# The order of work in a two-layer attention and GLU kernel: a list for two steps, maxima in halves, the transposed maxima ahead of PV, wo's products in the filler

## The chip, the core and the metric

The kernel runs on one core of one Trainium2 chip. The metric is the device time of one execution in microseconds. Three executions of the kernel before took 2374.63, 2372.8 and 2376.28 us, so the median is 2374.63 us. A core has TensorE for matrix products (PE in the profile, with its weight loads listed as PEld), VectorE (DVE), ScalarE (ACT), GpSimd (POOL) and SyncE (SP), which here only issues transfers. Each engine takes its instructions in the order in which the program lists them; an instruction that waits holds up what stands behind it on its engine.

## The reference

Two layers, each of attention with sixteen query heads and one key and value head, and of a gated unit. S is 2048, D 448, a head 28 wide, F 1792.

```python
def _A_ref(x, wq, wk, wv, wo):
    q = (x @ wq).reshape(B, S, H, Dh).transpose(0, 2, 1, 3)
    k = x @ wk
    v = x @ wv
    scores = jnp.einsum("bhqd,bkd->bhqk", q, k) * (Dh ** -0.5)
    p = _softmax(scores, axis=-1)
    o = jnp.einsum("bhqk,bkd->bhqd", p, v)
    return o.transpose(0, 2, 1, 3).reshape(B, S, H * Dh) @ wo
...
x = A_x
x = x + _A_ref(_layernorm(x), A_wq, A_wk, A_wv, A_wo)
x = x + _B_ref(_layernorm(x), B_w_gate, B_w_up, B_w_down)   # (sigmoid(x wg) * (x wu)) wd
x = x + _A_ref(...)
x = x + _B_ref(...)
```

## The kernel before

A unit u is 128 queries; a layer has 16 units. For each unit the kernel goes over 16 blocks of 128 keys, and one such block is a **step**, so that a layer has 256 steps and the program 512. I number steps from 0 in each layer.

In a step, `scores` (L485) makes four products `s`, one for each group of four heads, into one bank of PSUM each, and ACT writes the exponential `P` of each. `pv` (L494) multiplies the four `P` of the step before by the values (`pv`, summed over the 16 steps of the unit). Softmax needs the maximum over all keys of each query and head before a unit's first score, so `mx_gen` (L442) runs ahead: its group of four products `mx` (L458) takes one group of heads against 512 keys, and DVE reduces each of the four banks to a column of `mp` (L462). Sixteen groups make a unit. Then DVE reduces `mp` to `m32` and scales it to `m16` (L471, L472), and `fin` (L474) turns `m16` with TensorE (`mt`, L477), copies it (`mr`, L479) and stores it as a row of the unit's queries `QS`, from which the scores take it as a further term of the product. `fin` is put on the list `late`; with LT = 1 it runs in the same call of the generator that made `m16`, ahead of the next group's first product.

What TensorE does besides is **filler**: a list of generators (`Filler`, L727) with the query projections (`qp`), the gated unit's products (`gp`, `up`, `dn`) and, run whole and not in slices, a unit's output projection `wo` (twelve products, `fc`, L584) and the key and value projection (`kv`). `slice` (L743) first calls `flush`, which emits work that was deferred (evictions and the like), then adds nanoseconds to a debt and emits products until their estimated cost has paid it. The main loop sets `rate` in each step: what is left of the filler over the steps until it must be done.

The order inside a step is a string:

```python
    ORDER = "FSFSFSFSPXM"
    MORE = (5, 10)
```

F is a slice of the filler with a quarter of `rate`, S one score, P the products with the values, M one group of maxima (two in steps 5 and 10 of a layer's first unit), and X calls `tick`, which starts the next stage of the work that follows a unit: f0 to fb (sums, reciprocals and scaling through DRAM and POOL), `fc` with `wo`, then layer norm (fd), its transposed copy (fe) and the block's filler (ff). `fc` runs inside `tick` by `fill.run`, so its twelve products stand between P and M.

PSUM tiles of the pool `psf` share seven banks: `s`, `mx`, `qp`, `gp`, `up`, `dn`, `wo`, `mt` and `kv` all have the tag "f". `pv` has a bank of its own. A product into a bank waits until the tile that held it before was read.

Of the kernel before, what the change touches and what calls it, by code (L numbers as in the profile page):

```python
# [19 lines left out]
def interleaved_layers_kernel(ctx: ExitStack, tc: tile.TileContext, x, wq, wk, wv, wo, wg, wu, wd, out, layers=2):  # L20
# [421 lines left out]
    def mx_gen(l):  # L442

        load_qh(l, 0)
        for u in range(U):
            qh = QH[l, u]
            mp = wk1.tile([128, 4, 4, NB], F32, name="mp", bufs=2)
            for kb in range(NB):
                for g in range(G):
                    for i in range(len(late) - 1, -1, -1):  # L450
                        late[i][0] -= 1
                        if late[i][0] <= 0:
                            late.pop(i)[1]()
                    assert KVD[l] >= 4 * (kb + 1)
                    ps = [psf.tile([128, 512], F32, tag=BANKS["m"], name="mx", bufs=NBK[BANKS["m"]])
                          for _ in range(4)]
                    for h in range(4):
                        nc.tensor.matmul(ps[h], qh[32 * h:32 * h + 32, g],  # L458
                                         KK[l][32 * h:32 * h + 32, 1, kb * 512:(kb + 1) * 512], start=True,
                                         stop=True, tile_position=(32 * h, 0))  # L460
                    for h in range(4):
                        nc.vector.tensor_reduce(mp[:, g, h, kb:kb + 1], ps[h], axis=AX.X, op=OP.max)  # L462
                    ps = None
# [5 lines left out]
            m32 = wk1.tile([128, 16], F32, name="m32")  # L469
            m16 = wk1.tile([128, 16], F16, name="m16")  # L470
            nc.vector.tensor_reduce(m32, mp.rearrange("p g h k -> p (g h) k"), axis=AX.X, op=OP.max)  # L471
            nc.vector.tensor_scalar(m16, m32, -(2.0 ** -15), None, op0=OP.mult)  # L472

            def fin(u=u, m16=m16):  # L474
                stored.add(("m", l, u))
                p = fps([16, 128], F16, "mt")
                nc.tensor.transpose(p, m16, id16)  # L477
                r = wk1.tile([16, 128], F16, name="mr")
                nc.vector.tensor_copy(r, p)  # L479
                nc.gpsimd.dma_start(QS[l, u][28:29].rearrange("o g h n -> o (g h) n"), r)  # L480
            late.append([LT, fin])
# [44 lines left out]
    class Block:  # L526
# [8 lines left out]
        def tile(self, u):  # L535
# [47 lines left out]

            def fc():  # L584
                need(1)
                p = fps([128, D], F32, "wo")
                n = 0
                for h in range(4):
                    for a, c in ((0, 0), (0, 1), (1, 0)):
                        nc.tensor.matmul(p, v["oT"][:, a, h * 128:(h + 1) * 128], WO[:, c, h], start=n == 0, stop=n == 11)  # L590
                        n += 1
                        yield C448

                def f():
                    nc.vector.scalar_tensor_tensor(self.x1[:, t], p, osc, v["xr"], op0=OP.mult, op1=OP.add)
# [18 lines left out]
            def ff():  # L614
# [4 lines left out]
                        fill.add(qgen(l + 1, 1), G * QCH)  # L619
                return  # L620
                yield
            return (1, f0), (1, fx), (1, fy), (1, fz), (1, fw), (1, fa), (1, fb), (2, fc), (2, fd), (3, fe), (2, ff)

        def load_w(self, f):
            need(2 + f)
# [98 lines left out]
    QCH = 11 * C512  # L724
    BULK = FC * 22 * C256 + TB * 3 * FC * C448

    class Filler:  # L727
        def __init__(self):
            self.gens, self.debt = [], 0.0

        @property
        def left(self):
# [10 lines left out]
        def slice(self, ns):  # L743
            now[0] += 1
            flush()
            self.debt += ns
            while self.gens and self.debt > 0:
                g = self.gens[0]
                c = next(g[0], None)
                if c is None:  # L750
                    self.gens.remove(g)
                    continue
                self.debt -= c
                g[1] -= c
            if not self.gens:
                self.debt = min(self.debt, 0.0)

    fill = Filler()
# [65 lines left out]
    def first_mx():  # L824

        while QDONE.get((0, 0), 0) <= nmx % G and QDONE.get((0, 0), 0) < G:
            fill.slice(QCH / 2)
        next(mxs[0])

    for i in range(NT + L4):  # L830
        for k, f in st0:
# [38 lines left out]
    for l in range(layers):  # L870
# [10 lines left out]
        while late:  # L881
            late.pop(0)[1]()
        fill.slice(QCH)
        prevP = None
        rate = 0.0
        for step in range(U * KT):
            u, kt = divmod(step, KT)
            P = []
            for o in ORDER:
                if o == "S":  # L890
                    scores(l, u, kt, len(P), P)
                elif o == "M":
                    for _ in range(1 + (u == 0 and kt in MORE)):
                        next(mx, None)
                elif o == "P":
                    if prevP is not None:
                        pv(*prevP)
                elif o == "X":
                    if u and kt == 1:
                        b = (u - 1) // TB  # L900
                        if (l, b) not in BLK:
                            BLK[l, b] = Block(l, b)
                        later(*BLK[l, b].tile(u - 1))
                    if l == 0:
                        paced(step)
                    tick()
                    fed = sum(BLK[l, b].fed == TB for b in range(NBL) if (l, b) in BLK)
                    if fed < NBL - 1:
                        rate = fill.left / max(FIRST + TB * KT * fed - step, 1)
                    else:  # L910
                        rate = max(fill.left - KEEP, 0) / (U * KT - step)
                else:
                    fill.slice(rate / ORDER.count("F"))
            prevP = (l, u, kt, P)
        pv(*prevP)
# [5 lines left out]
        while (side or pend or fill.gens) if final else (side or pend or done < 4 * NB):  # L921
            tick()
            for _ in range(4):
                fill.slice(VS / 4)
            n += 1
            if not final and done < 4 * NB and QDONE.get((l + 1, 0)) == G and mx_ready(l + 1, done):
                if n >= 5 or done >= 4 * (NB - 1):
                    next(mxs[l + 1])
                    done += 1
                    n = 0  # L930

# [20 lines left out]
```

## Time and profile before

| what | value |
|---|---|
| median of three executions | 2374.63 us |
| span of the profiled execution, first to last instruction | 2370.5 us |
| steps 0 to 45 of layer 0 | 116.91 to 283.23 us |
| steps 46 to 255 of layer 0, up to the last steps | 283.23 to about 1133 us |
| the end of layer 0's units and blocks, start of layer 1 | about 1133 to 1284.45 us |
| steps 0 to 43 of layer 1 | 1284.45 to 1431.46 us |
| steps 44 to 255 of layer 1 | 1431.46 to 2283 us |
| the last blocks | 2283 us to the end |

The profile lists instructions of one execution with start and duration, and what ended the idle time before one, read from the semaphores. Its page gives no time of the profiled execution but its span; the 4.1 us between span and median lie before the first and after the last instruction, or are the spread between executions. A matrix product's listed duration contains the way through the array, so products that follow each other overlap: the time that one costs is the distance between starts.

### The profile page before, as it was taken

The page shows a single profiled execution, that of the slowest core. Times are in us where ns is not written, and L with a number is a line of the kernel's source. Part 1 is how long each engine was busy: PE and PEld are TensorE (multiplying, and loading weights), DVE is VectorE, ACT ScalarE, POOL GpSimd, SP SyncE. Part 2 cuts the span into 40 slices and gives each one's busy share as a digit, 9 for nine tenths or more (in the row PEclk, how much of TensorE's full clock was granted, in tenths as well). Part 3 has the DMA queues.
Part 4 walks back from the last instruction along what each step waited for, and adds up shares of the span by engine and source line. Part 5 has one row for each costly group of instructions (what it writes and reads, how often), then busy time and mean ns, then how long its engine had stood idle before and what let it go on. Part 6 is the DMA issues. An engine that isn't in the chain of part 4 may idle for free.

```text
span 2370.5 us, 40937 instructions
## 1 busy us (share of the span) xinstructions
PE 2226.5 (94%) x15592; PEld 990.3 (42%) x15592; DVE 1624.5 (69%) x2858; ACT 1560.6 (66%) x2583; POOL 348.7 (15%) x621
## 2 busy tenths in 40 slices
PE   3688899999999999999999989999999999999999
PEld 1221244444444444444573223444444444444456
DVE  3787787777767777774258887777677776777321
ACT  5497767676667767777513777767676776777751
POOL 5403565001111010101011011000000000000010
PEclk9899999999999999999999999999999999999999
DMA  5433563322223132322342112322232222222133
GB/s 145 132 115 95 155 197 111 102 85 71 90 70 108 55 101 85 91 94 63 108 136 57 27 49 82 95 63 87 62 106 63 89 63 91 86 81 93 57 109 120
DMA packets 227525, 218.57 MB, mean 92 GB/s; under 512 B 159408, under 2 KB 187760, under 8 KB 227328
## 3 DMA queue, kind: packets, MB, share of 16 engines
q1 hardware_dynamic: 220832, 200.11, 28.3%
q0 software_dynamic: 5376, 14.87, 1.7%
q8 instruction: 122, 2.00, 0.3%
q10 hardware_dynamic: 1120, 0.98, 0.1%
q14 instruction: 75, 0.61, 0.1%
HBM read 175.37 MB, written 23.59 MB: 84 GB/s over the span
## 4 chain that ended last, share of the span: by engine, by line
PE 78%; DVE 11%; ACT 3%; DMA 2%; issue 2%; SPq 1%; POOL 0%; ACTq 0%; DVEq 0%; POOLq 0%
PE pv L499 19%; PE s L488 16%; PE dn L680 11%; PE gp L334 10%; PE up L334 10%; DVE mp L462 8%; PE mx L458 6%; PE wo L590 3%; ACT P L491 2%; PE qp L334 2%; DVE st L289 0%; DMA qd<-qst 0%; DMA sums<-rc 0%; DMA lb<-sums 0%; DMA XT<-hl 0%
## 5 line engine op out<-in xcount | busy, mean ns | idle before, releaser
L491 ACT ACTIVATE P<-s,esc 128x512 f32<-128x512 f32 x2048 | 1309.2, 690 | 513.2 <-PE s L488 496.1
L462 DVE TENSOR_REDUCE mp<-mx 128x1 f32<-128x512 f32 x2048 | 1268.2, 683 | 408.0 <-PE mx L458 404.1
L488 PE MATMUL s<-QS,KK 96*128 96x512 f16 x2048 | 761.4, 382 | 61.8 <-DVE mp L462 41.1
L334 PEld LDWEIGHTS <-wgu 128*128 128x128 f16 x4928 | 458.1, 97 | 243.5 <-issue 96.8
L499 PE MATMUL pv<-P,VV 128*32 128x512 f32 x4096 | 549.2, 609 | 0.0
L334 PE MATMUL up<-XT,wgu 128*128 128x256 f16 x2464 | 375.6, 272 | 0.0
L334 PE MATMUL gp<-XT,wgu 128*128 128x256 f16 x2464 | 374.2, 273 | 0.2
L680 PE MATMUL dn<-WD,h 128*128 128x448 f16 x1344 | 321.7, 352 | 0.0
L488 PEld LDWEIGHTS <-KK 96*128 96x128 f16 x2048 | 193.1, 97 | 181.3 <-issue 107.9
L458 PE MATMUL mx<-KK,QH 32*128 32x512 f16 x2048 | 217.8, 389 | 17.3 <-DVE mp L462 5.3
L458 PEld LDWEIGHTS <-QH 32*128 32x128 f16 x2048 | 53.6, 91 | 396.8 <-issue 385.6
L680 PEld LDWEIGHTS <-h 128*128 128x128 f16 x1344 | 124.1, 98 | 135.8 <-issue 22.0
L499 PEld LDWEIGHTS pv<-P,VV 128*32 128x32 f32 x4096 | 81.0, 108 | 206.0 <-issue 193.9
L573 POOL TENSOR_TENSOR lb<-pvs,lb 128x512 f32<-128x512 f32 x32 | 40.5, 1265 | 789.0 <-DMA lb<-sums 647.5
L654 ACT ACTIVATE h<-th 128x512 f16<-128x512 f32 x112 | 70.4, 629 | 86.0 <-DVE th L651 85.8
L295 POOL TENSOR_SCALAR rs<-mv 128x1 f32<-128x1 f32 (+2 forms) x53 | 13.4, 252 | 702.4 <-DVE mv L290 691.6
L651 DVE SCALAR_TENSOR_TENSOR th<-th,up 128x512 f32<-128x512 f32 x112 | 76.1, 679 | 56.9 <-PE up L334 44.4
L334 PE MATMUL qp<-XT,WQ 128*128 128x512 f16 x352 | 108.7, 409 | 2.5 <-DVE mp L462 1.2
L655 DVE SCALAR_TENSOR_TENSOR h<-th,h 128x512 f16<-128x512 f32 x112 | 78.8, 703 | 46.1 <-ACT h L654 46.1
L643 ACT ACTIVATE th<-gp,gsc 128x512 f32<-128x512 f32 x112 | 76.9, 687 | 45.8 <-PE gp L334 45.8
L590 PE MATMUL wo<-WO,oT 128*128 128x448 f16 x384 | 78.3, 353 | 0.2 <-DVE oT L580 0.2
L334 PEld LDWEIGHTS <-WQ 128*128 128x128 f16 x352 | 34.0, 102 | 61.3 <-issue 38.8
(117 smaller groups left out, 787.8 us busy)
## 6 DMA issues: line engine op xcount, KB each, us to landing
wgu<-wgu_d SPq DMA_DIRECT2D x224, 512.0 KB
QS<-qd SPq DMA_DIRECT2D x384, 32.0 KB
lb<-sums SPq DMA_DIRECT2D x128, 64.0 KB
xr<-in_A_x_dram SPq DMA_DIRECT2D x32, 224.0 KB
qd<-qst POOLq DMA_DIRECT2D x28, 256.0 KB, 2.6
wgu_d<-sgu POOLq DMA_DIRECT2D x14, 512.0 KB, 3.8
QH<-qd SPq DMA_DIRECT2D x28, 128.0 KB
x2d<-x SPq DMA_DIRECT2D x16, 224.0 KB
```

Source lines behind the costliest of these rows:

```text
L334: nc.tensor.matmul(ps, a, b, start=n == 0, stop=n == 10)
L458: nc.tensor.matmul(ps[h], qh[32 * h:32 * h + 32, g], KK[l][32 * h:32 * h + 32, 1, kb * 512:(kb + 1) * 512], start=True, stop=True, tile_po ...
L462: nc.vector.tensor_reduce(mp[:, g, h, kb:kb + 1], ps[h], axis=AX.X, op=OP.max)
L488: nc.tensor.matmul(s, KK[l][0:96, 0, kt * 128:(kt + 1) * 128], QS[l, u][:, g].rearrange("p h n -> p (h n)"), start=True, stop=True)
L491: nc.scalar.activation(p, s, AF.Exp, scale=esc)
L499: nc.tensor.matmul(v[32 * g:32 * g + 32], VV[l][:, kt], P[g], start=kt == 0, stop=kt == KT - 1, tile_position=(0, 32 * g))
L590: nc.tensor.matmul(p, v["oT"][:, a, h * 128:(h + 1) * 128], WO[:, c, h], start=n == 0, stop=n == 11)
L643: defer(lambda: nc.scalar.activation(th, gp.rearrange("p j n -> p (j n)"), AF.Tanh, scale=gsc))
L651: nc.vector.scalar_tensor_tensor(t, th, 1.0, up.rearrange("p j n -> p (j n)"), op0=OP.add, op1=OP.mult)
L654: nc.scalar.activation(h[:, 0], t, AF.Copy, scale=2.0 ** -17)
L655: defer(lambda: nc.vector.scalar_tensor_tensor(h[:, 1], t, 2.0 ** -17, h[:, 0], op0=OP.mult, op1=OP.subtract), 1)
L680: nc.tensor.matmul(p, hs[f // 2][:, a, o:o + 128], WD[:, f, c], start=n == 0, stop=n == 3 * FC - 1)
```

## The change

The string becomes one of two, each for two steps, chosen by the rate when the pair begins:

```diff
-    ORDER = "FSFSFSFSPXM"
+    FULL = "FSFSFSFSTPXMFSFSFSFSTPXM"
+    LEAN = "FSFSmFSFSTPXmFSFSmFSFSTPXm"
+    PLAG = 1
+    LEANR = 600.0
...
+        while step < U * KT:
+            order = FULL if rate > LEANR else LEAN
+            for o in order:
...
                 elif o == "M":
-                    for _ in range(1 + (u == 0 and kt in MORE)):
-                        next(mx, None)
+                    group(mx)
+                elif o == "m":
+                    next(mx, None)
+                elif o == "T":
+                    finish()
                 elif o == "P":
-                    if prevP is not None:
-                        pv(*prevP)
+                    if len(PQ) > (sn % 4 == 0) * PLAG:
+                        pv(*PQ.pop(0))
                 elif o == "X":
+                    if u == 0 and kt in MORE:
+                        group(mx)
```

The maxima's generator now stops after two products and their reductions; `group` calls it twice. The unit's last reductions go with its sixteenth group, and the turning waits on `late` for T, which stands ahead of P:

```diff
+                    for hh in (0, 2):
+                        ps = {h: psf.tile([128, 512], F32, tag=BANKS["m"], name="mx", bufs=NBK[BANKS["m"]])
+                              for h in (hh, hh + 1)}
...
+                        if hh == 0:
+                            yield
...
+                    if kb * 4 + g == 15:
+                        maxima(l, u, mp)
                     yield
...
+    def maxima(l, u, mp):
+        m32 = wk1.tile([128, 16], F32, name="m32")
+        m16 = wk1.tile([128, 16], F16, name="m16")
+        nc.vector.tensor_reduce(m32, mp.rearrange("p g h k -> p (g h) k"), axis=AX.X, op=OP.max)
+        nc.vector.tensor_scalar(m16, m32, -(2.0 ** -15), None, op0=OP.mult)
...
+        late.append(fin)
+
+    def finish():
         while late:
-            late.pop(0)[1]()
+            late.pop(0)()
+
+    def group(m):
+        next(m, None)
+        next(m, None)
```

The output projection becomes a generator that stands first in the filler, and its later stages are put on the list when it has ended:

```diff
             def fc():
                 need(1)
+                fill.first.append(wo())
+                return
+                yield
+
+            def wo():
                 p = fps([128, D], F32, "wo")
...
                 defer(f)
+                later((2, fd), (3, fe), (2, ff))
...
+            for _ in range(DEAL):
+                while self.first:
+                    c = next(self.first[0], None)
+                    if c is not None:
+                        self.debt -= c
+                        break
+                    self.first.pop(0)
             while self.gens and self.debt > 0:
```

DEAL is 100, so that one slice takes all twelve products.

With the numbers that the program computes for `rate`, LEAN orders steps 0 to 45 of layer 0 and steps 0 to 43 of layer 1, and FULL all others. The lists of ACT and SP keep their order. Three places show what moves.

First place, TensorE in a lean step, step 30 of layer 1. Before, the scores stand together, and the values' products and four maxima's products follow:

```order
L488 LDWEIGHTS KK
L488 MATMUL s<-QS,KK 128x512
L488 LDWEIGHTS KK
L488 MATMUL s<-QS,KK 128x512
L499 MATMUL pv<-P,VV 32x512 x4
L458 LDWEIGHTS QH
L458 MATMUL mx<-KK,QH 128x512
L458 LDWEIGHTS QH
L458 MATMUL mx<-KK,QH 128x512
```

Now, from the second score of that step on:

```order
L497 LDWEIGHTS KK
L497 MATMUL s<-QS,KK 128x512
L455 LDWEIGHTS QH
L455 MATMUL mx<-KK,QH 128x512
L455 LDWEIGHTS QH
L455 MATMUL mx<-KK,QH 128x512
L497 LDWEIGHTS KK
L497 MATMUL s<-QS,KK 128x512
L497 LDWEIGHTS KK
L497 MATMUL s<-QS,KK 128x512
L508 MATMUL pv<-P,VV 32x512 x4
```

Two of the four products of the maxima moved from behind `pv` to between the second and the third score.

Second place, TensorE around an output projection in a full step, step 57 of layer 1. Before, the projection follows `pv`, and this is its end (the last of twelve products, then the maxima and the next step's score):

```order
L590 LDWEIGHTS oT
L590 MATMUL wo<-WO,oT 128x448
L458 LDWEIGHTS QH
L458 MATMUL mx<-KK,QH 128x512
L458 LDWEIGHTS QH
L458 MATMUL mx<-KK,QH 128x512
L458 LDWEIGHTS QH
L458 MATMUL mx<-KK,QH 128x512
L458 LDWEIGHTS QH
L458 MATMUL mx<-KK,QH 128x512
L488 LDWEIGHTS KK
L488 MATMUL s<-QS,KK 128x512
```

Now the beginning of the projection stands behind the same four products:

```order
L508 MATMUL pv<-P,VV 32x512 x4
L455 LDWEIGHTS QH
L455 MATMUL mx<-KK,QH 128x512
L455 LDWEIGHTS QH
L455 MATMUL mx<-KK,QH 128x512
L455 LDWEIGHTS QH
L455 MATMUL mx<-KK,QH 128x512
L455 LDWEIGHTS QH
L455 MATMUL mx<-KK,QH 128x512
L604 LDWEIGHTS oT
L604 MATMUL wo<-WO,oT 128x448
```

The twelve products moved past the group of maxima, to the first slice of the next step; its four scores follow them.

Third place, TensorE where a unit's maxima are turned in a full step, step 61 of layer 1. Before, `mt` stands behind the values' products:

```order
L488 LDWEIGHTS KK
L488 MATMUL s<-QS,KK 128x512
L499 MATMUL pv<-P,VV 32x512 x4
L477 LDWEIGHTS m_18083
L477 MATMUL mt<-id_79,m_18083 16x128
L458 LDWEIGHTS QH
L458 MATMUL mx<-KK,QH 128x512
```

Now it stands ahead of them:

```order
L497 LDWEIGHTS KK
L497 MATMUL s<-QS,KK 128x512
L480 LDWEIGHTS m_18045
L480 MATMUL mt<-id_79,m_18045 16x128
L508 MATMUL pv<-P,VV 32x512 x4
L455 LDWEIGHTS QH
L455 MATMUL mx<-KK,QH 128x512
```

On DVE the two reductions that make `m16` stand behind the sixteenth group's four in both programs, in this step as their next neighbours; in steps where other work of DVE stood between, they now come before it.

More of the change, by code (lines that the diff above doesn't have):

```diff
@@ L725, in interleaved_layers_kernel @@
     BULK = FC * 22 * C256 + TB * 3 * FC * C448
+    DEAL = 100
     class Filler:
@@ L729, in __init__ @@
             self.gens, self.debt = [], 0.0
+            self.first = []
         @property
@@ L754, in slice @@
                 g[1] -= c
-            if not self.gens:
+            if not self.gens and not self.first:
                 self.debt = min(self.debt, 0.0)
@@ L827, in first_mx @@
             fill.slice(QCH / 2)
-        next(mxs[0])
+        group(mxs[0])
     for i in range(NT + L4):
@@ L911, in interleaved_layers_kernel @@
                         rate = max(fill.left - KEEP, 0) / (U * KT - step)
+                    step += 1
                 else:
-                    fill.slice(rate / ORDER.count("F"))
-            prevP = (l, u, kt, P)
-        pv(*prevP)
+                    fill.slice(rate * 2 / order.count("F"))
+        while PQ:
+            pv(*PQ.pop(0))
         flush(True)
@@ L920, in interleaved_layers_kernel @@
         n = done = 0
-        while (side or pend or fill.gens) if final else (side or pend or done < 4 * NB):
+        while (side or pend or fill.gens or fill.first) if final else (side or pend or fill.first or done < 4 * NB):
             tick()
@@ L927, in interleaved_layers_kernel @@
                 if n >= 5 or done >= 4 * (NB - 1):
-                    next(mxs[l + 1])
+                    group(mxs[l + 1])
                     done += 1
```

64 lines of the change are left out of this document (29 added, 35 removed).

## Prediction
> **What bounds the kernel now.** The shares of the page are means over stages with different limits, so I read busy time by stage first, then TensorE's waits by stage, then the order of time at the places that the change touches. These rows give busy time by stage: start and end, length, then PE, PEld, DVE, ACT and POOL with their instructions, TensorE's clock, the DMA share and GB/s.
>
> ```profile
> 116.91:283.23 166.32, 139.14 (x793) 33.02 (x792) 133.04 (x230) 133.76 (x237) 45.35 (x51) 0.95 0.39 115
> 283.23:1133.00 849.77, 828.62 (x5972) 373.79 (x5971) 615.47 (x1078) 599.79 (x976) 147.25 (x251) 1.00 0.32 96
> 1284.45:1431.46 147.01, 132.99 (x783) 33.31 (x782) 121.28 (x205) 111.49 (x185) 12.46 (x24) 0.99 0.12 35
> 1431.46:2283.00 851.54, 841.01 (x6028) 380.68 (x6030) 589.28 (x1013) 605.12 (x967) 62.87 (x134) 1.00 0.26 81
> ```
>
> Rows two and four are the full steps: TensorE is busy 828.6 of 849.8 us and 841.0 of 851.5, VectorE and ScalarE about 70%. Whatever TensorE waits there is lost, and nothing else counts. Rows one and three are the lean steps, 46 in 166.3 us and 44 in 147.0 us. No engine is full; VectorE is idle for 33.3 and 25.7 us, so 59 us is the most that a better order can win there. These rows are followed by TensorE's waits in the two full stages (sum in us, times, longest):
>
> ```profile
> PE s L488 <- DVE mp L462: 13.8, 35, 0.9
> PE mt L477 <- DVE m L472: 2.8, 6, 1.2
> ...
> PE s L488 <- DVE mp L462: 8.5, 26, 0.5
> ```
>
> The scores wait for banks that the maxima hold, some 60 times in all. Where that is comes out in the order of time.
>
> **wo behind the maxima (full steps).** This is step 57 of layer 1: start, duration, engine, line, instruction, and idle time ahead of it.
>
> ```profile
> 1481.84 1.06 PE L499 MATMUL pv<-P,VV 128*32 128x512 f32 x8
> 1482.84 2.44 PE L590 MATMUL wo<-WO,oT 128*128 128x448 f16 x12
> 1485.21 0.39 PE L458 MATMUL mx<-KK,QH 32*128 32x512 f16 x4
> 1485.54 0.39 PE L488 MATMUL s<-QS,KK 96*128 96x512 f16 x1
> 1485.64 2.48 DVE L462 TENSOR_REDUCE mp<-mx 128x1 f32<-128x512 f32 x4 [3.73 <-PE mx L458]
> 1485.97 0.69 ACT L491 ACTIVATE P<-s,esc 128x512 f32<-128x512 f32 x1 [3.27 <-PE s L488]
> 1486.38 0.38 PE L488 MATMUL s<-QS,KK 96*128 96x512 f16 x1 [0.45 <-DVE mp L462]
> 1486.98 0.59 PE L488 MATMUL s<-QS,KK 96*128 96x512 f16 x2 [0.22 <-DVE mp L462]
> 1487.50 1.06 PE L499 MATMUL pv<-P,VV 128*32 128x512 f32 x8
> 1488.04 0.68 DVE L595 SCALAR_TENSOR_TENSOR x<-wo,osc,xr 128x448 f32<-128x448 f32 x1
> 1488.50 0.39 PE L458 MATMUL mx<-KK,QH 32*128 32x512 f16 x4
> ```
>
> VectorE stands idle for 3.73 us while TensorE does `wo`, and then TensorE waits for VectorE, because the filler's debt is negative after `wo` and nothing stands between the scores. From the maxima's products to the next `pv` it takes 1487.50 - 1485.21 = 2.29 us. Now the maxima come first: `mx` at 1482.84, `wo` from 1483.17 to 1485.54, then four scores 0.21 apart (the last row of two scores: 0.59 - 0.38), so `pv` at 1486.50 and the next `mx` at 1487.50, 1.00 us sooner. The four reductions run from 1483.27 to 1485.75 beside `wo`. The fourth score needs the third, done by about 1485.2, and the next `mx` at 1487.50 needs the eviction of `wo`, 0.68 us from 1485.75. What is late next is ScalarE: its four exponentials still start at 1485.97 and end 2.4 us later, while the step after wants their banks 0.3 us earlier than they are free, at worst. I take 0.1 off and count 0.9 us. There are 24 such places, twelve in each layer: **-21.6 us**. The ends: 1.0 each, -24; or the waits that the profile lists, 0.67, less that 0.3, so -9.
>
> **The turned maxima ahead of pv (full steps).** Step 61 of layer 1, then two rows each of step 77 of layer 1 and of the first and last such step of layer 0:
>
> ```profile
> 1496.34 2.48 DVE L462 TENSOR_REDUCE mp<-mx 128x1 f32<-128x512 f32 x4
> 1498.86 1.07 PE L499 MATMUL pv<-P,VV 128*32 128x512 f32 x8
> 1499.11 0.17 DVE L472 TENSOR_SCALAR m<-m 128x16 f16<-128x16 f32 x1
> 1499.74 0.22 PE L477 MATMUL mt<-id,m 128*16 128x128 f16 x1
> 1499.90 0.40 PE L458 MATMUL mx<-KK,QH 32*128 32x512 f16 x4
> ...
> 1561.52 2.48 DVE L462 TENSOR_REDUCE mp<-mx 128x1 f32<-128x512 f32 x4 [1.73 <-PE mx L458]
> 1564.30 1.07 PE L499 MATMUL pv<-P,VV 128*32 128x512 f32 x8
> ...
> 347.18 2.47 DVE L462 TENSOR_REDUCE mp<-mx 128x1 f32<-128x512 f32 x4
> 349.42 1.06 PE L499 MATMUL pv<-P,VV 128*32 128x512 f32 x8
> ...
> 1091.77 2.48 DVE L462 TENSOR_REDUCE mp<-mx 128x1 f32<-128x512 f32 x4 [1.74 <-PE mx L458]
> 1094.74 1.06 PE L499 MATMUL pv<-P,VV 128*32 128x512 f32 x8
> ```
>
> This part speaks against the change. `m16` is ready at 1499.28, and TensorE reached `pv` at 1498.86. Behind `pv` the turning found its operand ready; ahead of it TensorE must wait to about 1499.34, and `pv` follows 0.16 us later as `mx` does now, at 1499.50: 0.64 later, less 0.04 that `mt` costs now. What is queued behind the waiting instruction is `pv`, the next maxima and so VectorE's next work. As a rule, `pv` is late by the end of the four reductions plus 0.68 us, less its own start: 0.65 in step 61, 0.38 in step 77, 0.91 in step 61 and 0.19 in step 237 of layer 0. In layer 1 six units are of the first kind, six of the second, and the unit at the border to the lean steps loses about 1.0: +6.7. Layer 0's twelve lose 0.1 to 1.0, about 5.5 in sum, and give up the waits of today, 2.8 by the list and 4.0 by distances between starts: +1.5. Together **+8 us**; the ends are +3 (only waits that VectorE shows above half a microsecond) and +12.
>
> **The lean steps.** Maxima in halves feed VectorE twice in a step. But a step's length is a chain, seen in step 31 of layer 1:
>
> ```profile
> 1387.88 0.39 PE L458 MATMUL mx<-KK,QH 32*128 32x512 f16 x4
> 1388.20 0.60 PE L488 MATMUL s<-QS,KK 96*128 96x512 f16 x2
> 1389.05 0.38 PE L488 MATMUL s<-QS,KK 96*128 96x512 f16 x1 [0.23 <-DVE mp L462]
> 1389.64 0.38 PE L488 MATMUL s<-QS,KK 96*128 96x512 f16 x1 [0.22 <-DVE mp L462]
> 1389.95 1.06 PE L499 MATMUL pv<-P,VV 128*32 128x512 f32 x8
> 1390.95 0.39 PE L458 MATMUL mx<-KK,QH 32*128 32x512 f16 x4
> ```
>
> The third and fourth score wait for the banks of the first and second maximum of the group before; then `pv` 0.31 later and `mx` 1.00 later: 3.07 us. The two last products of a group make the same chain when two others went earlier, so halves alone win nothing; what counts is which bank the fourth score gets. I followed each PSUM bank's previous tile in both built programs. Over the 90 lean steps, the chain of two maxima holds 35 steps before and 15 after; a fourth score that waits for the first exponential of its own step 16 and 36; third and fourth both on exponentials 4 and 7. The rest are mixed. By the rows above the second kind takes 0.32 us to the first score, 0.43 to its exponential (step 57, 1485.54 to 1485.97), 0.69 for it, some 0.04 to the fourth score, then 0.31 and 1.00: 2.79 us. The third kind takes 3.43, the distance of the first two rows below, which are exponentials of steps 31 and 32 of layer 0. The last two rows stand around a doubled group in layer 1.
>
> ```profile
> 225.19 2.42 ACT L491 ACTIVATE P<-s,esc 128x512 f32<-128x512 f32 x4
> 228.62 2.42 ACT L491 ACTIVATE P<-s,esc 128x512 f32<-128x512 f32 x4 [1.01 <-PE s L488]
> ...
> 1298.74 2.42 ACT L491 ACTIVATE P<-s,esc 128x512 f32<-128x512 f32 x4 [0.70 <-PE s L488]
> 1308.54 2.42 ACT L491 ACTIVATE P<-s,esc 128x512 f32<-128x512 f32 x4 [1.75 <-PE s L488]
> ```
>
> So 20 steps win 0.28 us (-5.6) and three lose 0.36 (+1.1). The two steps with a doubled group take 9.80 us where two plain ones take 6.14; six products in a row instead of eight free TensorE one pair of reductions sooner, about 1.2 us, at four places, of which the two of layer 0 lie beside a ScalarE that is nearly full: -3. The four lean projections win about half a microsecond each: -2. Sum **-9.5 us**, ends +8 (all steps gated as the mixed ones) and -22.
>
> A pair costs TensorE almost what four cost, since the four run side by side: four take 0.39, and a fifth on the same rows makes 0.60, as this row shows.
>
> ```profile
> 152.03 0.60 PE L458 MATMUL mx<-KK,QH 32*128 32x512 f16 x5
> ```
>
> That is 0.21 us more in each lean step, 90 x 0.21 = 19 us. I count it at nothing: the middle pair stands ahead of a third score that waits for the first reduction anyway, until 1.17 us after the pair before (1387.88 to 1389.05); the cover is gone where that score finds a free bank. The Trainium skill, "TensorE: Matmul & The Clock Gate", Part 3 (Packing small matmuls), gives a pack's span as one product's duration plus about 4 ns for each further tile, so two packs of two cost two spans. By that rule, taken alone, the sum would be those 19 us higher; the trace agrees with the price and not with its place on the path.
>
> **The sum.** -21.6 + 8 - 9.5 = -23.1 us. On the profiled execution's span of 2370.5 that is 2347.4; the median lies 4.1 above that span, so **2352 us**, rounded up.
>
> **The rivals.**
> 1. The halves also keep VectorE fed: a lean step falls to its four reductions, 2.48 us. With 59 us of idle there as the limit and ScalarE nearly full in layer 0's first 25 steps, some 37 are won in place of 9.5: 2324 us. For it: VectorE's idle is all waiting for `mx`. Against it: the fourth score's bank. Chance 0.10.
> 2. The middle pair is on TensorE's path: +19, so 2371 us. For it: TensorE shows 133 of 147 us busy. Against: the 0.23 and 0.22 us waits in step 31, room enough. The Trainium skill's span rule, named above, would have it so. Chance 0.15.
> 3. wo's waits come back behind it, as scores that wait for exponentials: 0.3 won and not 0.9, 14 us less, 2366 us. For: ScalarE's start does not move. Against: only two scores need those banks. Chance 0.12.
> 4. **Slower:** the exponential's gate. If ScalarE is behind by one exponential whenever the fourth score waits for the first, those 36 steps take 3.43 and not 2.79, 23 us, and the 15 and the 32 mixed ones, which come out of step with it, 0.36 more each, 17 us: 2392 us. It decides once the lean steps lose more than 13.6 us against now, 0.15 each. For: steps of 3.43 exist. Against: ScalarE is idle for 1.01 us even in such a step, by the row at 228.62. Chance 0.07.
> 5. That the change does not do what it says is excluded by the built program: all three moves stand in it.
>
> **How the numbers follow.** The forecast has the other 0.56. About 5 us (0.2%) is what a measurement of this kernel tells from no change. Rivals 2 and 3 lie between 2360 and 2374, one third of them within that bound: same 0.09, slower 0.06, faster 0.85. The range runs from 2334 (lean steps at their best, or wo at its upper end) to 2369, which leaves out most of rival 1, all of rival 4 and a third of 2 and 3, 0.2 in sum.
>
> **What would show it.** Right: `s` waiting for `mp` in the full stages falls from 22.3 us to a few; `mt` waits for `m16` at some 20 places there, 0.2 to 0.7 us each; VectorE's reductions start about 0.4 us after `mx` and run beside `wo`; lean stages of about 163 and 140 us. Wrong: `mt` without waits, `s` waiting for `P` for more than 5 us behind `wo`, or lean stages as long as before.

## The result, and the profile after

The changed kernel takes **2345.49 us** (median of four executions, 2344.46 to 2350.7). The kernel before took 2375.45 (four executions, 2372.8 to 2378.89). The ratio is 0.9879, with a 95% interval of 0.9862 to 0.9895: faster by 1.2%. The profiled execution took 2345.36 us, 1.8 more than its span:

```profile
span 2343.6 us, 40936 instructions
```

The busy times of the four stages, as for before: start and end, length, PE, PEld, DVE, ACT, POOL with their instructions, TensorE's clock, DMA share, GB/s. The ends of rows two and four are the moments at which the same instructions stand as at 1133 and 2283 us before.

```profile
115.64:276.67 161.03, 149.03 (x793) 33.69 (x793) 132.57 (x229) 133.35 (x237) 42.55 (x49) 0.96 0.41 118
276.67:1118.31 841.64, 824.65 (x5972) 374.46 (x5971) 616.63 (x1078) 597.61 (x976) 149.35 (x252) 1.00 0.33 97
1269.94:1412.91 142.97, 139.70 (x783) 33.66 (x783) 122.64 (x208) 111.30 (x185) 12.48 (x24) 0.99 0.13 35
1412.91:2255.47 842.56, 836.91 (x6028) 380.96 (x6030) 590.11 (x1010) 601.50 (x967) 62.82 (x134) 1.00 0.27 82
```

The full stages fell by 8.1 and 9.0 us, the lean ones by 5.3 and 4.0: 26.4 of the 26.9 us by which the spans differ. TensorE does the same products in both. In the full stages its idle time fell by 4.2 and 4.9 us, and its listed busy time by 4.0 and 4.1. The second should be waiting too: a score is listed with 0.38 us but costs 0.21 when another follows at once (0.59 for two), so a wait behind it stands in part under busy. What waits are left there, layer 0 first, then layer 1 (sum in us, times, longest):

```profile
PE s L497 <- ACT P L500: 6.0, 6, 3.5
PE s L497 <- DVE mp L459: 5.7, 15, 1.1
PE mt L480 <- DVE m L475: 3.5, 6, 0.7
...
PE mt L480 <- DVE m L475: 4.7, 13, 1.3
PE s L497 <- DVE mp L459: 0.2, 1, 0.2
```

The scores' waits for banks of the maxima fell from 22.3 to 5.9 us; in layer 1, where they were 26 waits, one is left. The turning now waits for `m16` at 19 places, 8.2 us in sum, where it waited at 7, 3.2 us; and in layer 0 there is one new wait of 3.5 us for an exponential.

**wo behind the maxima**, step 57 of layer 1 (start, duration, engine, line, instruction):

```profile
1463.19 1.07 PE L508 MATMUL pv<-P,VV 128*32 128x512 f32 x8
1464.19 0.40 PE L455 MATMUL mx<-KK,QH 32*128 32x512 f16 x4
1464.52 2.44 PE L604 MATMUL wo<-WO,oT 128*128 128x448 f16 x12
1464.61 2.49 DVE L459 TENSOR_REDUCE mp<-mx 128x1 f32<-128x512 f32 x4 [1.35 <-PE mx L455]
1466.80 1.03 PE L497 MATMUL s<-QS,KK 96*128 96x512 f16 x4
...
1467.22 4.84 ACT L500 ACTIVATE P<-s,esc 128x512 f32<-128x512 f32 x8 [3.17 <-PE s L497]
1467.76 1.07 PE L508 MATMUL pv<-P,VV 128*32 128x512 f32 x8
...
1471.26 1.07 PE L508 MATMUL pv<-P,VV 128*32 128x512 f32 x8
```

VectorE reduces from 1464.61 to 1467.10 beside `wo`, and the four scores follow `wo` without a wait. From `pv` to `pv` it is 4.57 us, where it was 5.66 (1481.84 to 1487.50). The next step takes 3.50, where it took 3.46, so next to nothing comes back there: ScalarE runs eight exponentials in a row from 1467.22, and nobody on TensorE waits for them.

**The turning ahead of pv**, step 61 of layer 1:

```profile
1478.84 0.38 PE L497 MATMUL s<-QS,KK 96*128 96x512 f16 x1
1479.15 0.22 DVE L474 TENSOR_REDUCE m<-mp 128x16 f32<-128x64 f32 x1
1479.40 0.17 DVE L475 TENSOR_SCALAR m<-m 128x16 f16<-128x16 f32 x1
1479.63 0.22 PE L480 MATMUL mt<-id,m 128*16 128x128 f16 x1 [0.41 <-DVE m L475]
1479.64 1.07 PE L508 MATMUL pv<-P,VV 128*32 128x512 f32 x8
```

TensorE waits 0.41 us, much as foreseen. But `pv` starts 0.01 us behind `mt`, not 0.16.

**A wait that was not foreseen**, steps 46 to 48 of layer 0, the first full steps:

```profile
277.40 0.55 POOL L483 DMA_DIRECT2D QS<-mr  x1 [2.92 <-DVE mr L482]
281.31 1.15 POOL L142 TENSOR_TENSOR sgu<-rgu,sgu 128x512 f16<-128x512 f32 x1
282.49 0.72 ACT L129 ACTIVATE sgu<-rgu,swb 128x512 f16<-128x512 f32 x1 [3.40 <-POOL sgu L142]
283.84 0.59 PE L497 MATMUL s<-QS,KK 96*128 96x512 f16 x1 [3.47 <-ACT P L500]
```

`sgu` is the preparation of the gated unit's weights, dealt out step by step to GpSimd, ScalarE and VectorE; it is begun at X, just ahead of `tick`. With T ahead of X, GpSimd's issue of `QS<-mr` stands ahead of its share of `sgu` and waits 2.92 us for `mr`. So `sgu` is late, ScalarE waits 3.40 us for it in front of the exponentials, and TensorE 3.47 for these. Three engines pass on one wait, and TensorE's clock falls behind it (rows further below). Steps 46 to 61 take 72.59 us where they took 69.79.

### The profile page after: what moved, and what is told of

It is laid out like the page before. It is cut to its first block, busy times and chain, and to the rows that moved or that the text cites. A ratio compares the mean times of both kernels' runs of the same rounds, so it can differ in the third digit from the quotient of the medians.

```text
span 2343.6 us, 40936 instructions
## 1 busy us (share of the span) xinstructions
PE 2235.5 (95%) x15592; PEld 992.1 (42%) x15592; DVE 1628.0 (69%) x2858; ACT 1554.2 (66%) x2583; POOL 347.7 (15%) x621
## 4 chain that ended last, share of the span: by engine, by line
PE 81%; DVE 7%; ACT 3%; DMA 3%; issue 2%; POOL 2%; SPq 2%; ACTq 0%; POOLq 0%; DVEq 0%
PE pv L508 20%; PE s L497 17%; PE dn L695 11%; PE gp L334 10%; PE up L334 10%; PE mx L455 7%; DVE mp L459 5%; PE wo L604 3%; PE qp L334 2%; ACT P L500 2%; DMA XT<-hl 1%; SPq L419 0%; DMA lb<-sums 0%; DMA sums<-rc 0%; PE mt L480 0%
## 5 line engine op out<-in xcount | busy, mean ns | idle before, releaser
L497 PE MATMUL s<-QS,KK 96*128 96x512 f16 x2048 | 750.2, 382 | 26.7 <-ACT P L500 14.1
L455 PE MATMUL mx<-KK,QH 32*128 32x512 f16 x2048 | 251.7, 388 | 14.8 <-DMA QH<-qd 3.7
L455 PEld LDWEIGHTS <-QH 32*128 32x128 f16 x2048 | 60.9, 91 | 462.4 <-issue 453.1
```

Source lines behind the costliest of these rows:

```text
L455: nc.tensor.matmul(ps[h], qh[32 * h:32 * h + 32, g], KK[l][32 * h:32 * h + 32, 1, kb * 512:(kb + 1) * 512], start=True, stop=True, tile_po ...
L497: nc.tensor.matmul(s, KK[l][0:96, 0, kt * 128:(kt + 1) * 128], QS[l, u][:, g].rearrange("p h n -> p (h n)"), start=True, stop=True)
```

## The experiments

Each was run in three rounds beside the kernel before. A ratio is to before; "against the changed kernel" is the difference from 2345.49. The kernel before had medians of 2373.4 to 2375.7 us in these rounds, so differences of 2 us between kernels of different rounds say nothing. The table gives stages of the profiled executions in us, by the first exponential of a step. "First" is the time to the first step, where all programs are nearly alike, "between" the end of layer 0 up to layer 1's first step.

| kernel | first | layer 0: 0–45 | 46–61 | 62–253 | between | layer 1: 0–43 | 44–253 | rest |
|---|---|---|---|---|---|---|---|---|
| before | 116.91 | 166.32 | 69.79 | 801.06 | 130.38 | 147.01 | 845.84 | 93.16 |
| changed | 115.64 | 161.03 | 72.59 | 790.13 | 130.55 | 142.97 | 836.86 | 93.78 |
| wo alone | 118.25 | 166.12 | 69.12 | 789.15 | 132.98 | 144.54 | 832.46 | 93.79 |
| without wo | 118.72 | 162.33 | 73.88 | 802.92 | 131.94 | 143.63 | 849.55 | 93.51 |
| no lean string | 116.22 | 166.65 | 68.19 | 789.70 | 130.47 | 149.19 | 837.27 | 93.11 |
| T behind P | 118.45 | 160.79 | 72.68 | 784.74 | 132.13 | 141.61 | 831.96 | 93.55 |
| T behind X | 117.86 | 157.96 | 66.98 | 786.50 | 131.75 | 141.39 | 832.00 | 93.27 |
| lean everywhere | 116.56 | 160.52 | 71.40 | 848.85 | 131.08 | 141.70 | 906.85 | 94.20 |
| fb later | 115.44 | 161.43 | 69.89 | 794.58 | 132.27 | 141.50 | 840.06 | 93.24 |
| T behind X, fb later | 118.06 | 158.56 | 68.69 | 791.79 | 131.72 | 141.69 | 837.22 | 93.24 |
| pair later | 116.58 | 160.76 | 66.83 | 786.48 | 132.39 | 144.27 | 832.02 | 93.77 |
| pairs even | 118.49 | 162.71 | 65.94 | 786.49 | 131.58 | 146.88 | 831.96 | 93.66 |

"First" spreads over 3 us though next to nothing differs there; a difference of a few microseconds between two sums of a row says nothing, one of a stage does.

### wo alone, and the change without it

The kernel before with one part of the change:

```diff
             def fc():
                 need(1)
+                fill.first.append(wo())
+                return
+                yield
+
+            def wo():
...
```

> The kernel before with one edit alone: wo's twelve products stand first in the next slice of the filler, behind the group of maxima. Theory (wo's wait is the largest term): in the full steps each of 24 places wins 1.07 us, the distance between two pv that the profile of the changed kernel shows, and the lean ones about half a microsecond each, so 26 to 28 us less than before, about 2348 us, ratio 0.988 to 0.990. Rival (the waits come back behind wo, or the gain is the halves'): 0.3 us at each place, 7 us, 2368 us.

And the changed kernel without that part:

```diff
-                fill.first.append(wo())
-                return
-                yield
+                yield from wo()
```

> The changed kernel with wo run whole inside the step's tick again, ahead of the maxima; all else as changed. Theory: it loses what the edit alone wins, 24 to 28 us against the changed kernel, so 2370 to 2373 us and a ratio to before of 0.998 to 0.999. Rival (halves and the early turning carry the gain): it keeps two thirds of the gain, 2355 us.

wo alone: 2342.71 us (2340.37 to 2348.19), ratio 0.9862, interval 0.9844 to 0.988. Without wo: 2378.57 us, ratio 1.0018, interval 1.0007 to 1.0029. One part makes 32.8 us, the other parts together cost 3.1, and the sum, -29.7, is what the whole change does (-30.0): no interaction shows.

The full stages of the changed kernel without that part:

```profile
281.05:1136.77 855.72, 829.18 (x5972) 373.27 (x5971) 616.09 (x1078) 599.48 (x976) 148.67 (x252) 1.00 0.32 95
1433.42:2288.66 855.24, 841.48 (x6028) 379.75 (x6030) 587.47 (x1010) 604.71 (x967) 62.84 (x134) 1.00 0.27 81
```

1710.96 against 1684.20 us with it: 26.8, over 24 places 1.1 us each. The same places measured from `pv` to `pv`, together with the step behind, give 1.07 on the mean (most go from 5.66 to 4.56 or 4.57, and the step behind takes 0.01 to 0.1 longer): 25.7. The medians show more, 33.1 and 32.8; of these 3.1 stand ahead of the first step in the profiled execution of the changed kernel without wo, and wo alone's own executions spread over 8 us.

### No lean string

```diff
-    LEANR = 600.0
+    LEANR = -1.0
```

> The changed kernel with the full string in all steps. Theory (the lean string shortens the lean steps by 9 us and gives 6 of them back in layer 0 where ScalarE waits for POOL's weights): 3 to 5 us more than the changed kernel, 2349 us; layer 1's lean stage as long as before, 147 us instead of 143. Rival (the lean string's gain is whole): 9 us more, 2354 us. Rival (halves cost TensorE what they win): 2345 us or less.

2355.19 us (2352.57 to 2362.17), ratio 0.9916, interval 0.9896 to 0.9936: 9.7 us slower than the changed kernel. The lean string is worth about what the prediction gave it, but the place differs. The lean stages of this kernel:

```profile
116.22:282.87 166.65, 138.80 (x793) 33.47 (x792) 132.68 (x229) 133.23 (x237) 43.94 (x51) 0.95 0.39 114
1271.23:1420.42 149.19, 136.04 (x783) 33.87 (x782) 122.07 (x207) 111.02 (x186) 12.52 (x25) 0.95 0.12 34
```

By stages the string wins 5.6 and 6.2 us, and 4.4 of it go in steps 46 to 61, where this kernel takes 68.19 and the changed one 72.59: the wait of 3.47 us. In layer 1 part of this may be the clock's, which is 0.95 in the stage above and 0.99 in the changed kernel's. T stands ahead of X here too, and still the long wait does not come:

```profile
281.56 0.54 POOL L483 DMA_DIRECT2D QS<-mr  x1 [1.40 <-DVE mr L482]
```

The issue waits 1.40 us for `mr`, not 2.92, and ScalarE 1.35 and not 3.40. So it is T ahead of X and the lean string together that make the wait of 3.47 us.

### T behind P

```diff
-    FULL = "FSFSFSFSTPXMFSFSFSFSTPXM"
-    LEAN = "FSFSmFSFSTPXmFSFSmFSFSTPXm"
+    FULL = "FSFSFSFSPTXMFSFSFSFSPTXM"
+    LEAN = "FSFSmFSFSPTXmFSFSmFSFSPTXm"
```

> The changed kernel with T behind P in both strings: the maxima are still reduced with their sixteenth group, and only the turning moves behind the values' products. Theory (the turning ahead of pv holds TensorE up): the waits of mt for m16 go, 4.7 us in layer 1 and about 3.8 in layer 0, so 8 us less than the changed kernel, 2337 us; the last step's distance of two pv in step 61 of layer 1 falls from 4.43 to 3.95. Rival (the wait only moves, since the row of the scores is stored later and the scores wait for it, or POOL's list is held up longer): 2345 us or more.

2337.5 us (2333.25 to 2338.92), ratio 0.9834, interval 0.9818 to 0.9849: 8.0 us faster than the changed kernel. Steps 62 to 253 of layer 0 fall by 5.4 us and steps 44 to 253 of layer 1 by 4.9, the latter as much as the turning waits there in the changed kernel (4.7). Step 61 of layer 1 takes 3.94 us from `pv` to `pv`, where the changed kernel takes 4.43; 3.95 was expected. Steps 46 to 61 stay at 72.7: behind P the issue still stands ahead of `sgu`.

### T behind X

```diff
-    FULL = "FSFSFSFSTPXMFSFSFSFSTPXM"
-    LEAN = "FSFSmFSFSTPXmFSFSmFSFSTPXm"
+    FULL = "FSFSFSFSPXTMFSFSFSFSPXTM"
+    LEAN = "FSFSmFSFSPXTmFSFSmFSFSPXTm"
```

> The changed kernel with T moved behind X in both strings, so that the turned maxima stand behind pv and behind the tick, as close to the order of before as the list allows. Two theories on the 3.40 us that ScalarE's sgu waits for GpSimd's sgu in steps 46 to 48 of layer 0. Theory A (GpSimd's queue): the issue QS<-mr stands ahead of sgu in GpSimd's order and waits 2.92 us for mr; behind the tick it stands behind sgu, the scores' 3.47 us wait goes, and steps 46 to 61 of layer 0 fall from 72.6 (changed kernel) and 72.7 us (T behind pv) to 68 to 70, as before (69.8); the time falls by 2 to 5 us against T behind pv, to 2332 to 2336. Theory B (the clock): these steps are longer because TensorE has more filler to do right there after the lean string, whatever GpSimd's order; then the stage stays at 72 to 73 and the time within 2 us of T behind pv, 2337.5. Against the changed kernel (2345.5), both expect at least 6 us less, since full steps no longer wait for m16.

**2330.59 us** (2327.02 to 2332.89), ratio 0.9809, interval 0.9795 to 0.9824, by the median the fastest of all: 14.9 us less than the changed kernel. Theory A holds in kind, and more was won than it gave (2332 to 2336 us, and 68 to 70 in steps 46 to 61). GpSimd, ScalarE and TensorE at the same place:

```profile
277.05 1.16 POOL L142 TENSOR_TENSOR sgu<-rgu,sgu 128x512 f16<-128x512 f32 x1
278.25 0.72 ACT L129 ACTIVATE sgu<-rgu,swb 128x512 f16<-128x512 f32 x1
279.12 0.52 POOL L483 DMA_DIRECT2D QS<-mr  x1
```

The issue stands behind `sgu` and waits for nothing; ScalarE doesn't wait either, and steps 46 to 61 take 66.98 us, 5.6 less. That is more than the wait of 3.47: the clock behind it stays up, and 0.6 of it stands at the turning in step 61. The same four windows of the two kernels show it (changed kernel first, then T behind X; the clock is the number behind POOL's):

```profile
252.00:256.00 4.00, 3.52 (x13) 0.43 (x12) 2.26 (x4) 2.16 (x4) 3.53 (x4) 0.55 0.49 138
256.00:260.00 4.00, 4.00 (x15) 0.59 (x13) 2.73 (x6) 3.63 (x6) 1.31 (x2) 0.50 0.93 238
...
280.00:284.00 4.00, 0.53 (x3) 0.20 (x2) 0.75 (x1) 1.51 (x3) 3.57 (x4) 0.89 0.34 74
284.00:288.00 4.00, 4.00 (x16) 0.59 (x15) 3.33 (x6) 1.74 (x3) 3.70 (x3) 0.50 0.30 121
```

```profile
252.00:256.00 4.00, 1.56 (x8) 0.47 (x6) 2.62 (x5) 1.61 (x4) 2.61 (x2) 1.00 0.56 154
256.00:260.00 4.00, 3.76 (x22) 0.90 (x25) 3.56 (x7) 3.63 (x7) 3.53 (x4) 1.00 0.49 138
...
280.00:284.00 4.00, 3.48 (x21) 0.97 (x21) 3.98 (x8) 2.06 (x4) 3.82 (x3) 1.00 0.72 198
284.00:288.00 4.00, 3.41 (x26) 1.34 (x24) 1.33 (x4) 3.97 (x8) 0.74 (x2) 1.00 0.72 234
```

In the changed kernel the granted clock is 0.50 in two stretches, behind a wait that ends at 252.47 and behind the one that ends at 283.84. With T behind X it is 1.00 throughout. The second stretch went with its wait. The first did not: TensorE still idles in window 252 to 256 (1.56 of 4 us busy), and yet the clock stayed. So of the 3.1 us that steps 0 to 45 gained, the move of T is not shown to be the cause.

### Stage fb one tick later

```diff
-            return (1, f0), (1, fx), (1, fy), (1, fz), (1, fw), (1, fa), (1, fb), (2, fc)
+            return (1, f0), (1, fx), (1, fy), (1, fz), (1, fw), (1, fa), (2, fb), (2, fc)
```

> The changed kernel with one edit: stage fb, which scales the unit's output by lb, is begun one tick later. In lean steps 39 to 41 of both kernels ScalarE's oT waits 2.73 us for GpSimd's lb, which waits for a transfer of the sums, and TensorE's clock falls after the wait (pv 1.94 us and wo 3.38 us in place of 1.06 and 2.44). Theory A: the wait is on the path and its after-effect too, about 3 us at each of the projections of the lean steps (four in all, two with the long wait seen): steps 0 to 45 of layer 0 fall from 161.0 to 156 to 159 us, steps 44 on unchanged, in sum 2 to 6 us less than 2345.5. Theory B: what follows (wo, layer norm, the filler of the block) is later by one step everywhere and some of it, at the ends of the layers, is on the path: the end of layer 0 (130.6 us) grows by up to one tick, 3 us, and the sum is within 2 us of 2345.5.

2352.86 us (2350.18 to 2354.91), ratio 0.9904, interval 0.9889 to 0.9918: 7.4 us slower than the changed kernel. Both theories fall. The wait was taken away: ScalarE's `oT` now waits 0.30 us for GpSimd's `lb`, not 2.73.

```profile
252.67 0.62 ACT L588 CAST oT<-lb 128x512 f16<-128x512 f32 x1 [0.30 <-POOL lb L582]
```

Yet steps 0 to 45 take 161.4 us, where the changed kernel takes 161.0. Steps 46 to 61 lose 2.7 us, and steps 62 to 253 of layer 0 and 44 to 253 of layer 1 grow, by 4.5 and 3.2. TensorE's waits in layer 0's full steps show part of it:

```profile
PE mt L480 <- DVE m L475: 5.9, 6, 3.2
PE s L497 <- DVE mp L459: 5.2, 17, 0.9
PE up L334 <- DVE mp L459: 2.8, 6, 0.6
```

The turning waits 5.9 us, not 3.5, and `up` waits where it did not. Everything behind `fb` is later by one step in each unit, and the reductions wait or are late in steps where they were not; that VectorE's share of the moved work (`oT`, the eviction of `wo`, the layer norm) makes them so is argued, not shown.

Both edits together:

> Both edits together, T behind X and fb one tick later. If the two waits are apart (one in steps 39 to 41, one in 46 to 48), the gains add: the time is that of T behind X less what fb later alone gives, within 1.5 us. If they are one (whichever comes first pushes the other), the sum is less than the parts by 2 us or more.

2346.26 us (2342.74 to 2347.14), ratio 0.9874, interval 0.9859 to 0.9888. By the sum of the parts it would be 2330.6 + 7.4 = 2338.0; it is 8 us more, so the parts are not independent. Steps 62 to 253 of layer 0 and 44 to 253 of layer 1 lose 5.3 and 5.2 us against T behind X; what else is lost was not followed.

### The lean string everywhere

```diff
-    LEANR = 600.0
+    LEANR = 1e9
```

> The changed kernel with the lean string in all 512 steps, so that each group of four products of the maxima goes as two pairs also in the 422 full steps, where TensorE is the bound. It tells what a pair costs there. Theory A (what the prediction took from the row of five products, and the Trainium skill's span rule): a second pack is 0.21 us more of TensorE, so 422 steps take 89 us more, 2434 us; full steps without wo go from 4.06 to 4.27 us on the mean. Theory B (the pair hides beside the scores' packs, which occupy other rows of the array): the steps take no more than now, 2340 to 2350 us. Between: by the mean distance of exponentials in steps 62 to 253 of layer 0 and 44 to 253 of layer 1 the price of a pair on the path.

2475.38 us (2472.95 to 2477.55), ratio 1.0423, interval 1.0406 to 1.0441: 129.9 us slower than the changed kernel. Theory B falls, and A had the price too low. The full stages:

```profile
277.08:1176.26 899.18, 895.62 (x5972) 375.82 (x5972) 626.03 (x1078) 602.46 (x976) 148.13 (x252) 1.00 0.31 91
1470.12:2382.67 912.55, 911.81 (x6028) 382.82 (x6031) 600.04 (x1010) 607.61 (x967) 62.62 (x134) 1.00 0.26 76
```

1811.73 us against 1684.20, 127.5 more, for 384 groups (764 and 772 products `mx` in these stages): 0.33 us per group, though TensorE is idle for only 3.6 and 0.7 us now, where it was 17.0 and 5.7. (The expectation counted 422 steps; at the end of a layer no group is due.) The price is seen between a score and the products behind it:

```profile
1605.29 0.38 PE L497 MATMUL s<-QS,KK 96*128 96x512 f16 x1
1605.51 0.54 PE L695 MATMUL dn<-WD,h 128*128 128x448 f16 x2
1605.88 0.38 PE L497 MATMUL s<-QS,KK 96*128 96x512 f16 x1
1606.20 0.39 PE L455 MATMUL mx<-KK,QH 32*128 32x512 f16 x2
1606.52 0.74 PE L695 MATMUL dn<-WD,h 128*128 128x448 f16 x3
```

A pair holds TensorE for 0.32 us (1606.20 to 1606.52), as long as four do (0.33: 1464.19 to 1464.52 in step 57 above). And a score in front of a pair costs 0.32 (1605.88 to 1606.20) where one in front of `dn` costs 0.22 (1605.29 to 1605.51). So splitting a group costs 0.4 us of TensorE. The prediction took 0.21 from a row of five products in a row; that fifth product came behind others on the same rows of the array, and showed neither of the two.

### Where the pair stands

On T behind X, the middle pair of the lean string one score later:

```diff
-    LEAN = "FSFSmFSFSPXTmFSFSmFSFSPXTm"
+    LEAN = "FSFSFSmFSPXTmFSFSFSmFSPXTm"
```

> T behind X, and the lean string's middle pair of the maxima between the third and the fourth score in place of between the second and the third. Theory A (banks): what sets a lean step is the fourth score, which in both programs gets the bank of the first exponential of its own step; the chain from the step's first score over that exponential to the fourth score, pv and the next pair, 2.8 to 3.0 us, stays, and the third score now waits for a reduction beside it. The lean stages stay at 158 us (layer 0, with T behind X) and 141.4 (layer 1) within 3 us each, the time at 2330.6 within 5 us. Theory B (supply): VectorE's reductions follow the pairs' places; with the pair one score later the reductions after it end up to 0.5 us later, and 90 steps lose some 0.2 us or more each: 2348 us or above. In both, the full steps are as with T behind X.

And both pairs moved:

```diff
-    LEAN = "FSFSmFSFSPXTmFSFSmFSFSPXTm"
+    LEAN = "FmSFSFSmFSPXTFmSFSFSmFSPXT"
```

> T behind X, and in the lean string both pairs moved: one ahead of the step's first score, behind a slice of the filler, one between the third and the fourth score. Theory A (banks): the fourth score still gets the bank of its own step's first exponential, which starts 0.3 us later, behind the pair: the lean stages stay at 158 and 141.4 us within 3 us each, the time at 2330.6 within 5 us. Theory B (supply): the second pair comes half a step after the first, the reductions need not wait for the next step's products, and a lean step falls to 2.5 to 2.7 us: 90 steps win 0.3 us each, 2305 us or less.

The pair later: 2332.52 us (2327.36 to 2343.79), ratio 0.9834, interval 0.9795 to 0.9873; its lean stages are longer by 2.8 and 2.9 us, 0.06 per step: within theory A's 3 us, and less than a third of what theory B gave. Even this is in part the clock, which is 0.50 from 254 to 262 us in this kernel and 1.00 there with T behind X. Pairs even: 2343.68 us (2339.53 to 2346.13), ratio 0.9874, interval 0.9858 to 0.9889. Theory B, which gave 2305 or less, falls: feeding VectorE evenly wins nothing. But the lean stages grew by 4.8 and 5.5 us, beyond A's 3 each. That the chain over the fourth score's bank sets these steps is thus supported, not settled; where the 10 us come from was not followed.

## Why the prediction was right, point by point

The forecast was 2352 us; 2345.5 came out, 6.5 less and within the range. Of this, 3.8 lies in the span (2347.4 against 2343.6), 2.2 in what lies around it (4.1 against 1.9 between this span and the median), the rest is rounding. That the sum came near is in part luck, since errors of both signs met:

| term | predicted | measured | by |
|---|---|---|---|
| wo behind the maxima | -21.6 | -25.7 to -26.8 | 24 places; without wo |
| turning ahead of pv, against before | +8 | +4.4 | distances from the fourth score to `mx` |
| lean steps | -9.5 | -9.3 | stages |
| steps 46 to 48 of layer 0 | none | about +5 | 3.47 us of wait and half a clock behind it; 5.6 with T behind X, less 0.6 at step 61's turning |

- **wo: the mechanism was right, the term mis-sized.** The step that failed is "I take 0.1 off and count 0.9 us". Next to nothing had to be taken off: ScalarE is late by eight exponentials in a row, and TensorE does not wait for it in the next step, which takes 3.50 us where it took 3.46. The place itself gives 1.09 (5.66 to 4.57), not 1.00. Each place wins 1.07 net, beyond the upper end of 1.0.
- **The turning: right in kind, half the size.** Layer 1 cost 4.7 and not 6.7 us, and layer 0 won 0.3 and did not lose 1.5. One part of the error is "`pv` follows 0.16 us later as `mx` does now"; it follows 0.01 later. The other is that gathering the unit's last reductions with the sixteenth group helps more than the prediction saw. The move of T alone costs more than the term: 8.0 us by the medians, 10.2 by the two full stages (1674.00 us with T behind P against 1684.20). The difference from +4.4 would be what the gathering gives. No run has the gathering alone; with T behind P, the distances from the fourth score to `mx` in layer 0 are 1.34 or 1.35 us at the turnings of its full steps, where before six of eleven were 1.5 to 2.7.
- **The lean steps: right in sum.** The stages were forecast at about 163 and 140 us and are 161.0 and 143.0. Without the string the lean steps of layer 1 take longer than before (149.19 us against 147.01), but at a clock of 0.95 against 0.99, so whether the turning costs them something is open; the string itself is worth 9.7 us by the medians. The pair's price was taken too low (0.21 for 0.4), but "I count it at nothing" held: in layer 1's lean stage TensorE is busy for 139.70 us where it was 132.99, and the stage is 4.0 shorter.
- **What was left out.** The prediction asked what stands behind `mt` on TensorE, and not what stands behind `QS<-mr` on GpSimd. There the moved step passed other work, and that cost about 5 us.

Of the rivals, the middle pair on TensorE's path is refuted for the lean steps and shown for the full ones, where the change does not use it. The Trainium skill, "TensorE: Matmul & The Clock Gate", Part 3 (Packing small matmuls), was right about the price: two further products in a pack cost 0.01 us by the rows of lean everywhere and step 57, and a second pack a whole span. Waits that come back behind wo as waits for exponentials are refuted by step 57 and by the sum of the parts. A lean step of 2.48 us did not come (142.97 us for 44 steps are 3.25 each), nor did it with pairs even. The exponential's gate with 3.43 us in every such step did not come: the lean stages fell.

The signs: waits for `mp` fell to a few, `mt` waits at 19 places, 0.4 us on the mean and 1.3 at most, the reductions start 0.42 us after `mx` (1464.19 to 1464.61): as said. A sign of error stood there too, scores that wait for `P` for more than 5 us in layer 0's full steps (6.0); 3.5 of these are the wait at 283.84, not behind `wo`.

## What to carry to other kernels

A long run of products is best placed right behind the products that feed another engine, so that this engine works beside it; count the full wait that goes, and look in the next step whether anything takes its place before taking some off. When a step moves, walk every queue into which it issues, the DMA issues too: the costliest single place here, about 5 us, was an issue that waits at the head of GpSimd's queue. Undo the parts of a bundle one at a time, since here one part brought as much as the whole, and the fastest version keeps it and puts the turning back.

## What the runs showed of the hardware that was not expected

- **A wait on TensorE costs more than its length where its clock falls.** These are the scores that end the wait in step 40 of layer 0, and the `pv` behind them, in the changed kernel and then with T behind X:

```profile
252.47 0.58 PE L497 MATMUL s<-QS,KK 96*128 96x512 f16 x1 [1.96 <-ACT P L500]
...
252.99 1.94 PE L508 MATMUL pv<-P,VV 128*32 128x512 f32 x8
```

```profile
255.94 0.38 PE L497 MATMUL s<-QS,KK 96*128 96x512 f16 x1 [1.62 <-ACT P L500]
256.24 1.07 PE L508 MATMUL pv<-P,VV 128*32 128x512 f32 x8
```

  In the first, the clock is 0.50 to about 262 us, with TensorE listed as busy for all of 256 to 264; in the second it stays at 1.00. These are the changed kernel's windows ahead of the fall and at its end:

```profile
248.00:252.00 4.00, 1.70 (x9) 0.55 (x8) 2.08 (x4) 1.26 (x3) 2.07 (x2) 1.00 0.54 159
...
260.00:264.00 4.00, 4.00 (x19) 1.65 (x16) 1.98 (x3) 0.00 (x0) 0.00 (x0) 0.67 0.71 256
```

  The Trainium skill, "TensorE: Matmul & The Clock Gate", Part 1 (The HAM clock gate), has the clock at half after an idle window of some 3.4 us and back after a busy one, the windows running free of the program. The half agrees. The idle window agrees with the fall at the wait of 3.47 us, but not with this one: no wait ahead of it is longer than 1.96 us, and TensorE is listed as busy for 1.70 of the 4 us before. Nor does the return agree, which took some 10 us of busy time here. That waits of 1.96 and 1.62 us end differently would fit windows that run free, but no run here shows that they are the cause.
- **Two products side by side cost TensorE what four cost**, 0.32 and 0.33 us, and the score ahead of the two costs 0.32 us, where it costs 0.22 ahead of `dn`.
